# A gated mix of linear attention and a squared-ReLU block: another way to sum the keys over the partitions

## The chip, the cores and the metric

One core of one Trainium2 chip. The metric is the device time of one execution in microseconds (us). The kernel before takes 435.01 us, the median of three runs (434.67, 435.01 and 435.04).

## The reference, cut to what is computed

Everything is float32. `x` is 2048 tokens by 448 features, there are 16 heads of 28 features, and the hidden layer has 1792 units.

```python
g = sigmoid((x * gate_w).sum(-1, keepdims=True))
q, k, v = split(x @ wqkv)                        # 16 heads of 28
phi = lambda t: where(t > 0, t + 1, exp(t)) + 1e-6
pq, pk = phi(q), phi(k)
kv = einsum("bhsd,bhse->bhde", pk, v)
z  = einsum("bhsd->bhd", pk)                     # the sum of the keys over all tokens
num = einsum("bhqd,bhde->bhqe", pq, kv)
den = einsum("bhqd,bhd->bhq", pq, z)[..., None] + 1e-6
a = (num / den) @ wo
h = relu(x @ w1 + b1) ** 2
b = h @ w2 + b2
return g * a + (1 - g) * b
```

The change is about `z`: 448 numbers, each a sum over 2048 tokens.

## The kernel before

Tokens are handled in four blocks of 512 (`b` from 0 to 3), hidden units in 14 tiles of 128 (`f` from 0 to 13). The kernel makes two passes over the blocks. The first pass (`for b in range(1, NB)`, with block 0 written out ahead of it) does hidden tiles 0 to 6. For each tile, `up` multiplies `x` by `w1` into the PSUM tile `h_ps`, `hidden` applies ReLU and the square (ACT, into `hr`) and splits the result into a high and a low half (DVE, into `hh` and `hl`), and `down` multiplies these by `w2` into `o_ps`, one tile later. Every float32 product is made from such halves: high by high, high by low, low by high.

In the same pass `keys` makes the keys of 128 tokens at a time, and POOL adds them up in `ksum`, 128 partitions by 448. So `ksum` holds, on each partition, the sum over those tokens that fell on this partition; what is left is a sum over the 128 partitions. `gram` makes products of `x` with the keys; DVE adds them up in the four tiles `gsum`. `z` itself is needed in the second pass as `zc`, 128 partitions by 4: a column of feature sums for each of the four groups `c` into which the query features are ordered.

`key_sums` is called in block 3 at `f == 5`. POOL lays `ksum` out anew in `zk` (L375 to L377), and the same function then computes the gates (`gate`, L379 to L382). `kv_product` is called when block 3 has done tile 7, the first of the second pass. Its first lines sum over the partitions on TensorE (PE): each of the four 128 by 128 pieces of `zk` is loaded as the weights (L398) and multiplied by a tile of ones two columns wide, `ones`. These are plain float32 products, which the profile shows as two weight loads and two matmuls each. L400 copies the result from PSUM into `zc`. Then come the sixteen products of `gsum` with the value weights `wv` (L404), their masked copy `kv_raw` (L407) and the second pass, where `queries` uses `zc` (L466, L468) for the denominators.

Order. PE, ACT and DVE run their instructions in the order of the program text (`manual_schedule`). The order on POOL's queue and on SP's, which issues nearly all loads (L58), is fixed when the kernel is built, by a planner with a cost model; each queue then runs in that order, and an instruction that waits holds up those behind it. Work tiles come from one pool of 15 slots of 2 KB a partition (`slot`), handed out anew as they come free, so an added tile moves later tiles to other slots and with it what they wait for. The PSUM tiles of tag "mm" take turns in two banks; `z_ps` is one of them.

The part of the loop where the call stands:

```python
            if b == 3:
                ...
                if f >= 3:
                    split_w2(NH + f - 3)
                if f == 5:
                    key_sums()
                if f >= 5:
                    load_kv(2 * f - 10)
                    load_kv(2 * f - 9)
```

Of the kernel before, what the change touches and what calls it, by code (L numbers as in the profile page):

```python
# [7 lines left out]
F = mybir.dt.float32  # L8
R = mybir.dt.float32r
AF = mybir.ActivationFunctionType  # L10
ALU = mybir.AluOpType
# [4 lines left out]
P = 128  # L16
# [6 lines left out]
NJ = D // JE  # L23
# [7 lines left out]
def gated_mix_kernel(ctx: ExitStack, tc: tile.TileContext, xw, xt, xn, wk, wq, wv, wo, w1a, w1b, w2, b1, b2, gw,  # L31
                     hmask, kvmask, halves, out):
    nc = tc.nc
    act, dve, pool, pe, sp = nc.scalar, nc.vector, nc.gpsimd, nc.tensor, nc.sync

    keep = ctx.enter_context(tc.tile_pool(name="keep", bufs=1))
# [7 lines left out]
    mm_p = ctx.enter_context(tc.tile_pool(name="mm_p", bufs=2, space=PSUM))  # L44
# [3 lines left out]
    def bank(name):  # L48
        turn[0] ^= 1
        return ms_p.tile([P, 512], F, name=name, tag=f"ms{turn[0]}")  # L50
# [3 lines left out]
    def slot(shape, dt, name):  # L54
        return work.tile(shape, dt, name=name, tag="s", bufs=NSLOT)

    def load(dst, src):
        sp.dma_start(out=dst, in_=src)  # L58
# [45 lines left out]
    def load_x(b, c):  # L104
        x_raw[b, c] = slot([P, TB], F, f"xr{b}_{c}")
        load(x_raw[b, c], xt[b, c])
# [4 lines left out]
    def split_x(b, c):  # L111
        if c == 0:
            xs[b] = new_x(b)
        (xh, xl), r = xs[b], x_raw[b, c]
        if c < 3:
            split_hi(act, xh[:, c], r)
            split_lo(dve, xl[:, c], r, xh[:, c])
        else:
            split_last(xh[:, 3], xl[:, 3], r, side)
# [28 lines left out]
    def load_w2(f):  # L148
        w2_raw[f] = slot([P, D], F, f"w2r{f}")
        load(w2_raw[f], w2[f])  # L150
# [8 lines left out]
    def load_xn(t):  # L159
        xn_raw[t] = slot([P, D], F, f"xnr{t}")  # L160
        load(xn_raw[t], xn[t])
# [28 lines left out]
        load_w1(0, 0, c)  # L190
    b1_s = keep.tile([P, NF], F, name="b1_s")
    half = keep.tile([P, 2], F, name="half")
    ones = keep.tile([P, 2], F, name="ones")
    logit = keep.tile([P, NT], F, name="logit")
    gate = keep.tile([P, 2, NT], F, name="gate")
    zc = keep.tile([P, 4], F, name="zc")
    load(b1_s, b1)
    load_w2(0)
    load_w2(1)
# [5 lines left out]
    b2_s = keep.tile([P, D], F, name="b2_s")  # L205
    gw_s = keep.tile([P, D], F, name="gw_s")
    hm = keep.tile([P, 8 + P], R, name="hm")[:, 8:]
    dve.memset(ones, 1.0)
    ksum = keep.tile([P, D], F, name="ksum")

    phase1 = ExitStack()
# [29 lines left out]
    def up(b, f):  # L241
        ps = mm_p.tile([P, 512], F, name=f"h_ps{b}_{f}", tag="mm")
        for c in range(4):
            up_chunk(ps, b, f, c)
        hidden(ps, b, f)
# [14 lines left out]
    def down(b, f, tiles=range(4), leave=0, end=NH - 1):  # L260
        h, lo = hs[f]
        w = w2_s[f]
        for i in tiles:
            if f % NH == 0:
                o_ps[i] = acc_p.tile([P, 512], F, name=f"o_ps{b}_{f}_{i}", tag="acc")
            cols = slice(i * P, (i + 1) * P)
            for n, (a, m) in enumerate([(h, w[:, 0]), (h, w[:, 1]), (lo, w[:, 0])]):
                owed.append((o_ps[i][:, :D], a[:, cols], m, f % NH == 0 and n == 0, f % NH == end and n == 2))
        pay(leave)

    def half_done(b):
        for i in range(4):
            dve.tensor_tensor(part[4 * b + i], o_ps[i][:, :D], b2_s, op=ALU.add)
# [56 lines left out]
    def gram(b, c):  # L330
        ps = bank(f"g_ps{b}_{c}")
        cs = slice(c * P, (c + 1) * P)
        terms = []
        for t in range(4 * b, 4 * b + 4):
            ph, pl, nh, nl = pend[t]
            terms += [(nh[:, cs], ph), (nh[:, cs], pl)] + ([(nl[:, cs], ph)] if c < 3 else [])
        products(ps[:, :D], terms)

        def after():
            if b == 0:  # L340
                gsum.append(tmp.tile([P, D], F, name=f"gsum{c}"))
                act.copy(gsum[c], ps[:, :D])
            else:
                dve.tensor_tensor(gsum[c], ps[:, :D], gsum[c], op=ALU.add)
        return [after]
# [5 lines left out]
    def load_wq(c):  # L351
        wq_raw[c] = slot([P, TB], F, f"wqr{c}")
        load(wq_raw[c], wq[c])
# [3 lines left out]
    def split_wq(c):  # L357
        raw = wq_raw.pop(c)
        split_hi(act, wq_s[:, c], raw)
        if c < 3:  # L360
            split_lo(dve, wq_s[:, 4 + c, :384], raw[:, :384], wq_s[:, c, :384])
        else:
            split_lo(dve, wq_s[64:, 3, :384], raw[64:, :384], wq_s[64:, 3, :384])
        second = [t[:, 384:].rearrange("p (j r) -> p j r", j=NJ)[:, :, 16:] for t in (wq_s[:, c], raw)]
        split_lo(dve, second[0], second[1], second[0])
# [1 line left out]

    zks = []  # L370

    def key_sums():
        zk = slot([P, 4, NJ, 32], F, "zk")
        ks = ksum.rearrange("p (j k) -> p j k", j=NJ)
        pool.memset(zk[:, 3], 0.0)  # L375
        pool.tensor_copy(zk[:, :3], ks[:, :, :96].rearrange("p j (c r) -> p c j r", c=3))
        pool.tensor_copy(zk[:, 3, :, :16], ks[:, :, 96:])  # L377
        zks.append(zk)
        act.activation(gate[:, 0], logit, AF.Exp, scale=-1.0)  # L379
        dve.tensor_scalar_add(gate[:, 0], gate[:, 0], 1.0)  # L380
        dve.reciprocal(gate[:, 0], gate[:, 0])
        dve.tensor_scalar(gate[:, 1], gate[:, 0], -1.0, 1.0, op0=ALU.mult, op1=ALU.add)  # L382
# [10 lines left out]

    def kv_product():
        kv_ps = bank("kv_ps")
        z_ps = mm_p.tile([P, 512], F, name="z_ps", tag="mm")
        for c in range(4):
            pe.matmul(z_ps[:, 2 * c:2 * c + 2], zks[0][:, c].rearrange("p j r -> p (j r)"), ones, start=True,  # L398
                      stop=True)
        dve.tensor_copy(zc, z_ps[:, 0:8:2])  # L400
        for j in range(NJ):
            js = slice(j * JE, (j + 1) * JE)
            for c in range(4):
                pe.matmul(kv_ps[:JE, js], wv_s[c][:, js], gsum[c][:, js], start=(c == 0), stop=(c == 3))  # L404
        raw = slot([P, D], F, "kv_raw")
        dve.memset(raw[96:], 0.0)
        dve.tensor_tensor(raw[:JE], kv_ps[:JE, :D], kvm[0], op=ALU.mult)  # L407
        return raw.rearrange("p (j k) -> p j k", j=NJ)
# [121 lines left out]
    def run_todo():  # L530
        now, todo[:] = sorted(todo, key=lambda step: step.__name__ == "join"), []
        for step in now:
            todo.extend(step() or ())
# [85 lines left out]
    for b in range(1, NB):  # L619
        for f in range(NH):  # L620
            leave = leaves[b][f]
            run_todo()
            up(b, f)
            if f == 0:
                down(b - 1, NH - 1)
                half_done(b - 1)
                if b == 1:
                    for c in range(1, 4):
                        todo += gram(0, c)
                        run_todo()  # L630
            else:
                down(b, f - 1, leave=leave)
            if f == 1:
                todo += late_keys
                run_todo()
            if f == 0:
                load_xn(4 * b)
            if f < 4:
                if f < 3:
                    load_xn(4 * b + f + 1)  # L640
                if f == 0 and leave:
                    late_keys = keys(4 * b, leave)
                else:
                    late_keys = []
                    todo += keys(4 * b + f)
            elif f < 6:
                todo += gram(b, f - 4)
            else:
                todo += gram(b, 2)
                run_todo()  # L650
                todo += gram(b, 3)
            if b + 1 < NB:
                if 1 <= f < 5:
                    load_x(b + 1, f - 1)
                if 3 <= f:
                    split_x(b + 1, f - 3)
            if b == 2:
                if f < 4:
                    load_wq(f)
                if 1 <= f < 5:  # L660
                    split_wq(f - 1)
                if f == 5:
                    raw = slot([P, P], F, "hmr")
                    pool.dma_start(out=raw, in_=hmask)
                    split_hi(act, hm, raw)
                    load(half, halves)
            if b == 3:
                if f < 4:
                    load_w1(1, 0, f)
                if f == 4:  # L670
                    for c in range(4):
                        split_w1(1, 0, c)
                if f >= 2:
                    load_w2(NH + f - 2)
                if f >= 3:
                    split_w2(NH + f - 3)
                if f == 5:
                    key_sums()
                if f >= 5:
                    load_kv(2 * f - 10)  # L680
                    load_kv(2 * f - 9)
# [160 lines left out]
```

## Time and profile before

| what | value |
| --- | --- |
| median of three runs | 435.01 us |
| profiled execution, first to last instruction (its span) | 432.7 us |
| what the median has beyond that span | 2.3 us |
| PE busy | 428.9 us, 99% of the span |
| DVE busy | 284.7 us, 66% |
| ACT busy | 174.8 us, 40% |
| POOL busy | 72.0 us, 17% |
| mean DMA rate | 67 GB/s |

The profile is of one further execution of the same program. PEld is the loading of weights into TensorE, which overlaps its matmuls. A row of the timeline gives the start in us, the busy time in us (of all instructions merged into the row), the engine, the line, the operation, output and input tiles, and shapes; in brackets the time that the engine stood idle before it and what ended that. A row of a window gives the stretch, its length, and the engine's busy time in it with the number of instructions. A row of the transfers gives the number of transfers, the size of one, and the median us from its issue to its landing. Line numbers are those of the kernel before.

### The profile page before, as it was taken

To read this page: it belongs to the slowest core of one execution; us is meant where nothing else is said; L and a number is where in the kernel's file an instruction comes from. 1 tells how busy PE (TensorE), PEld (TensorE's weight loads), DVE (VectorE), ACT (ScalarE), POOL (GpSimd) and SP (SyncE) were. 2 spreads that over 40 slices of the span, in tenths; PEclk is the share of its full clock that TensorE was granted. 3 is DMA by queue.
4 is the path that set the end of the run, shared out by engine and by line. 5 is a ranking of instruction groups with operands and counts; after the bars stand their busy time and mean duration, and the time that the engine had idled before them with its cause. 6 is when DMAs were issued, how large, how long until landed. Compare 5 with 4: busy or idle time off the path is not lost.

```text
span 432.7 us, 5576 instructions
## 1 busy us (share of the span) xinstructions
PE 428.9 (99%) x2058; PEld 380.6 (88%) x2058; DVE 284.7 (66%) x464; ACT 174.8 (40%) x304; POOL 72.0 (17%) x93
## 2 busy tenths in 40 slices
PE   9999999999999999999999999999999999999997
PEld 6889999898989899898898888988888888888986
DVE  5999518843499337884459777887653966457624
ACT  6855324521346133453145543444433534233421
POOL 0055006500065002540010441000100001000000
PEclk9999999999999999999999999999999999999999
DMA  8842302120232211223245321130101401002002
GB/s 284 240 134 63 96 0 71 24 68 5 65 89 63 68 45 48 66 59 110 65 117 144 72 63 38 63 120 0 26 0 46 139 0 27 0 0 86 0 2 85
DMA packets 18411, 29.11 MB, mean 67 GB/s; under 512 B 2896, under 2 KB 12736, under 8 KB 18384
## 3 DMA queue, kind: packets, MB, share of 16 engines
q1 hardware_dynamic: 16480, 26.46, 20.1%
q0 software_dynamic: 1760, 2.20, 2.3%
q8 instruction: 16, 0.26, 0.3%
q14 instruction: 11, 0.09, 0.1%
q10 hardware_dynamic: 144, 0.10, 0.1%
HBM read 22.43 MB, written 3.67 MB: 60 GB/s over the span
## 4 chain that ended last, share of the span: by engine, by line
PE 99%; DVE 0%; issue 0%
PE h_ps L229 32%; PE o_ps L254 31%; PE q_ps L84 8%; PE a_ps L84 8%; PE g_ps L84 8%; PE k_ps L254 8%; PE kv_ps L404 1%; PE warm_ps L177 1%; PE m_ps L84 1%; PE d_ps L84 0%; PE last L84 0%; PE h_ps L549 0%; PE z_ps L398 0%; DVE last L786 0%
## 5 line engine op out<-in xcount | busy, mean ns | idle before, releaser
L254 PE MATMUL o_ps<-w,hh 128*128 128x448 f32 x444 | 127.9, 362 | 0.0
L229 PE MATMUL h_ps<-xh,w 128*128 128x512 f32 x390 | 124.7, 390 | 0.0
L254 PEld LDWEIGHTS o_ps<-w,hh 128*128 128x128 f32 x444 | 83.2, 187 | 7.6
L229 PE MATMUL h_ps<-xl,w 128*128 128x512 f32 x224 | 86.7, 389 | 0.0
L229 PEld LDWEIGHTS h_ps<-xh,w 128*128 128x128 f32 x390 | 73.1, 188 | 14.7 <-DVE w L72 0.4
L254 PE MATMUL o_ps<-w,hl 128*128 128x448 f32 x222 | 80.4, 362 | 0.0
L233 ACT ACTIVATE hr<-h_ps,b_s 128x512 f32<-128x512 f32 x56 | 38.1, 680 | 85.8 <-PE h_ps L229 80.3
L69 DVE CAST hh<-hr 128x512 fp32r<-128x512 f32 x56 | 23.5, 420 | 61.3 <-ACT hr L234 61.1
L229 PEld LDWEIGHTS h_ps<-xl,w 128*128 128x128 f32 x224 | 42.0, 188 | 7.9
L254 PEld LDWEIGHTS o_ps<-w,hl 128*128 128x128 f32 x222 | 41.6, 188 | 3.7
L72 DVE TENSOR_TENSOR hl<-hr,hh 128x512 fp32r<-128x512 f32 x56 | 39.6, 707 | 3.4
L72 POOL TENSOR_TENSOR nl<-xnr,nh 128x384 fp32r<-128x384 f32 x16 | 17.2, 1075 | 119.0 <-ACT nh L65 118.9
L234 ACT ACTIVATE hr<-hr 128x512 f32<-128x512 f32 x56 | 35.4, 632 | 1.8
L84 PE MATMUL q_ps<-xh,wq_s 128*128 128x512 f32 x100 | 33.0, 389 | 0.0
L84 PE MATMUL a_ps<-m_s,qh 128*128 128x448 f32 x112 | 32.7, 362 | 0.0
L254 PE MATMUL k_ps<-wk_s,xh 128*128 128x448 f32 x112 | 32.7, 361 | 0.0
L475 POOL DMA_DIRECT2D qr<-qv x16 | 7.9, 503 | 124.3 <-ACT qv L472 94.5
L72 DVE TENSOR_TENSOR pl<-r,ph 128x448 fp32r<-128x448 f32 x16 | 23.7, 1479 | 0.0
L326 POOL TENSOR_TENSOR ksum<-ksum,r 128x448 f32<-128x448 f32 x15 | 23.3, 1554 | 1.1 <-DVE r L288 1.1
L84 PE MATMUL q_ps<-xl,wq_s 128*128 128x512 f32 x60 | 23.3, 389 | 0.0
L254 PE MATMUL k_ps<-wk_s,xl 128*128 128x448 f32 x64 | 23.2, 363 | 0.0
L84 PE MATMUL a_ps<-m_s,ql 128*128 128x448 f32 x64 | 23.2, 362 | 0.0
(118 smaller groups left out, 571.0 us busy)
## 6 DMA issues: line engine op xcount, KB each, us to landing
xr<-in_xt SPq DMA_DIRECT2D x27, 256.0 KB, 2.7
xnr<-in_xn SPq DMA_DIRECT2D x16, 224.0 KB, 2.6
out<-out SPq DMA_DIRECT2D x15, 224.0 KB, 2.0
w2r<-in_w SPq DMA_DIRECT2D x14, 224.0 KB, 2.7
w1r<-in_w1a SPq DMA_DIRECT2D x7, 256.0 KB, 2.8
w1r<-in_w1b SPq DMA_DIRECT2D x8, 192.0 KB, 3.3
m_s<-m POOLq DMA_DIRECT2D x12, 112.0 KB, 2.5
wqr<-in_wq SPq DMA_DIRECT2D x4, 256.0 KB, 2.7
```

Source lines behind the costliest of these rows:

```text
L69: eng.tensor_copy(hi, src)
L72: eng.tensor_tensor(lo, src, f32(hi), op=ALU.subtract)
L84: pe.matmul(out_ps, a, b, start=(i == 0), stop=(i == n - 1))
L177: pe.matmul(warm_ps[:, :256], warm[:, :P], warm, start=True, stop=True)
L229: pe.matmul(ps, a, m, start=(c == 0 and n == 0), stop=(c == 3 and n == 1))
L233: act.activation(r, ps, AF.Relu, bias=b1_s[:, f:f + 1])
L234: act.activation(r, r, AF.Square)
L254: pe.matmul(ps, a, m, start=start, stop=stop)
L326: pool.tensor_tensor(ksum, ksum, p, op=ALU.add)
L404: pe.matmul(kv_ps[:JE, js], wv_s[c][:, js], gsum[c][:, js], start=(c == 0), stop=(c == 3))
L475: pool.dma_start(out=r[p + 16:p + 32], in_=v[p:p + 16])
```

## The change

The four products with `ones`, the tile `z_ps` and the copy into `zc` go. In their place `key_sums` goes on, on DVE: it transposes each 32 by 32 block of `zk` into `zt` (128 by 512), and adds up the 32 values that now lie next to each other, so that each partition holds 16 sums over 32 partitions each. One transfer writes these to DRAM (`zd`, 512 pieces of 16 bytes), four transfers bring them back, one for each 32 partitions (`z4`, 128 pieces of 16 bytes each), so that the four partial sums of a feature lie on one partition. In the next tile, `add_z` adds them with two small DVE instructions. The layout of `zk` changes with it (POOL's three instructions stay), and the gates become a function of their own, called right behind.

In the built program, DVE's order is: the split of `w2` tile 9, transposition, addition, gates, `gsum[1]`, ..., `gsum[2]`, the split of `w2` tile 10, `add_z`, `gsum[3]`. SP's order is: the mask `kvm`, `wv[0]`, `wv[1]`, the store of `zd`, the four loads of `z4` (the first waits for the store to land), then `w2` tile 11, `wv[2]`, `wv[3]`. ACT's ReLU of tile 7 in block 3 writes a slot that `zk` held, and waits for the store of `zd`.

```diff
-    ones = keep.tile([P, 2], F, name="ones")
-    zc = keep.tile([P, 4], F, name="zc")
+    z4 = keep.tile([P, 4, 4], F, name="z4")
+    zc = z4[:, 0]
+    z_d = ctx.enter_context(tc.tile_pool(name="z_d", bufs=1, space=bass.MemoryType.DRAM))
-    dve.memset(ones, 1.0)
-    zks = []
     def key_sums():
-        zk = slot([P, 4, NJ, 32], F, "zk")
+        zk, zt = slot([P, NJ, 4, 32], F, "zk"), slot([P, 16, 32], F, "zt")
         ks = ksum.rearrange("p (j k) -> p j k", j=NJ)
-        pool.memset(zk[:, 3], 0.0)
-        pool.tensor_copy(zk[:, :3], ks[:, :, :96].rearrange("p j (c r) -> p c j r", c=3))
-        pool.tensor_copy(zk[:, 3, :, :16], ks[:, :, 96:])
-        zks.append(zk)
+        pool.memset(zk[:, :, 3], 0.0)
+        pool.tensor_copy(zk[:, :, :3], ks[:, :, :96].rearrange("p j (c r) -> p j c r", c=3))
+        pool.tensor_copy(zk[:, :, 3, :16], ks[:, :, 96:])
+        dve.transpose(zt.rearrange("p a s -> p (a s)"), zk.rearrange("p j c r -> p (j c r)"))
+        zr = zk.rearrange("p j c r -> p (j c r)")[:, :16]
+        dve.tensor_reduce(zr, zt, axis=mybir.AxisListType.X, op=ALU.add)
+        zd = z_d.tile([NJ, P, 4], F, name="zd")
+        load(zd.rearrange("j p c -> p j c"), zr.rearrange("p (j c) -> p j c", c=4))
+        for j in range(NJ):
+            load(z4[32 * j:32 * j + 32], zd[j].rearrange("(i r) c -> r i c", i=4))
+
+    def add_z():
+        dve.tensor_tensor(z4[:, :2], z4[:, :2], z4[:, 2:], op=ALU.add)
+        dve.tensor_tensor(zc, zc, z4[:, 1], op=ALU.add)
+
+    def gates():
         act.activation(gate[:, 0], logit, AF.Exp, scale=-1.0)
     def kv_product():
         kv_ps = bank("kv_ps")
-        z_ps = mm_p.tile([P, 512], F, name="z_ps", tag="mm")
-        for c in range(4):
-            pe.matmul(z_ps[:, 2 * c:2 * c + 2], zks[0][:, c].rearrange("p j r -> p (j r)"), ones, start=True,
-                      stop=True)
-        dve.tensor_copy(zc, z_ps[:, 0:8:2])
         for j in range(NJ):
 ...
                 if f == 5:
                     key_sums()
+                    gates()
+                if f == 6:
+                    add_z()
```

## The prediction

> **What bounds the kernel.** I read the page's busy times and its chain first, then the waits of PE, then the timeline of PE and its weight loads around the place of the change.
>
> ```profile
> span 432.7 us, 5576 instructions
> PE 428.9 (99%) x2058; PEld 380.6 (88%) x2058; DVE 284.7 (66%) x464; ACT 174.8 (40%) x304; POOL 72.0 (17%) x93
> PE 99%; DVE 0%; issue 0%
> PE warm_ps L177 <- PEq L834: 0.8, 1, 0.8
> ```
>
> PE is busy for 99% of the span, the chain that ended last runs through PE for 99%, and PE's waits hold one row only: 0.8 us at the very start. PE's stream has no hole that a better order elsewhere could close, so the time falls by what is taken out of the stream and rises by what makes PE wait. An edit on DVE, POOL or SP counts for nothing unless it makes PE wait.
>
> ```profile
> 216.29 0.39 PE L84 MATMUL q_ps<-xh,wq_s 128*128 128x512 f32 x1
> 216.51 0.95 PE L398 MATMUL z_ps<-ones,zk 128*128 128x2 f32 x8
> 217.32 3.38 PE L404 MATMUL kv_ps<-gsum,wv 128*112 128x112 f32 x32
> 220.47 0.48 PE L229 MATMUL h_ps<-xh,w 128*128 128x512 f32 x1
> 216.29 1.08 PEld L398 LDWEIGHTS z_ps<-ones,zk 128*128 128x128 f32 x8
> 216.52 0.19 PEld L398 LDWEIGHTS z_ps<-ones,zk 128*128 128x128 f32 x1
> 217.29 0.47 PEld L404 LDWEIGHTS kv_ps<-gsum,wv 128*112 128x112 f32 x4
> 217.32:220.47 3.15, 3.15 (x35) 1.00 0.47 145
> ```
>
> The eight matmuls of the key sums stand between the last query product and the `kv` products, from 216.51 to 217.32: 0.81 us. The `kv` products that follow take 3.15 us for 32, 0.098 each. The clock granted there is 1.00.
>
> **What goes.** A matmul two columns wide has almost nothing to stream; the weight loads set the pace. The first `z` load starts at 216.29, beneath the last query matmul, and costs nothing; the second starts only at 216.52; the first `kv` load starts at 217.29. Without `z`, the first `kv` load takes the free place at 216.29 and the second starts at 216.52. Before, the second `kv` load starts one step behind the first, at 217.29 + 0.098 = 217.39. So the `kv` loads, and all of PE behind them, come 217.39 - 216.52 = 0.87 us earlier. The plainer sum, first `kv` matmul from 217.32 to 216.51, gives 0.81. I take 0.87, since the loads set the pace, and keep 0.81 as the other end.
>
> The Trainium skill speaks against that saving in one place: "TensorE: Matmul & The Clock Gate", section "Back-to-back issue gap", lets matmuls of up to 64 columns follow each other after about 25 ns, which as an estimate makes the eight worth 0.2 us. The rows disagree with it: seven steps lead from the second `z` load at 216.52 to the first `kv` load at 217.29, 0.11 us each.
>
> DVE loses the `zc` copy and a memset at the start, neither on the chain. The bank of `z_ps` falls out of the turn of the "mm" banks; the next tile then waits for the one that was freed two tiles ago, as elsewhere.
>
> **What comes, on DVE.** Transposition, addition and `add_z` have no row before; these are the rows near them and the places that they land in.
>
> ```profile
> 199.38 0.17 DVE L380 TENSOR_SCALAR gate<-gate 128x16 f32<-128x16 f32 x1
> 200.93 0.62 DVE L344 TENSOR_TENSOR gsum<-g_ps,gsum 128x448 f32<-128x448 f32 x1 [0.89 <-PE g_ps L84]
> 204.80 0.43 DVE L69 CAST hh<-hr 128x512 fp32r<-128x512 f32 x1 [3.25 <-ACT hr L234]
> 205.26 0.69 DVE L72 TENSOR_TENSOR hl<-hr,hh 128x512 fp32r<-128x512 f32 x1
> 209.83 0.62 DVE L344 TENSOR_TENSOR gsum<-g_ps,gsum 128x448 f32<-128x448 f32 x1 [0.44 <-PE g_ps L84]
> 213.70 0.43 DVE L69 CAST hh<-hr 128x512 fp32r<-128x512 f32 x1 [3.25 <-ACT hr L234]
> 190.00 1.57 DVE L72 TENSOR_TENSOR pl<-r,ph 128x448 fp32r<-128x448 f32 x1
> 192.24 0.70 POOL L377 COPY zk<-ksum 128x64 f32<-128x64 f32 x1
> ```
>
> POOL has `zk` ready at 192.94, long before 199.38, where the transposition takes the place of the gates: it waits for nothing. On 128x512, DVE instructions take from 0.43 (the cast) to 0.69 (`hl`); the slowest large one here is 1.57 (while POOL is busy too). I take 0.69 each, as both new ones read all 512 values: 1.4 us, with ends 0.9 and 3.1. The sums are then ready at 200.8 (200.3 to 202.5). The gates and the second `gsum` addition move back by 1.4, less the 0.89 of idle ahead of that addition: about 0.5. The next work, `hh` at 204.80, comes after 3.25 us of idle, which swallows that, and the upper end too (199.38 + 3.1 + 0.7 for the gates + 0.62 = 203.8). Nothing on PE needs the late addition before the `kv` products. So: zero, by that idle time.
>
> `add_z` stands at 209.4, behind the split of a `w2` tile and ahead of the last `gsum` addition at 209.83. It is two instructions of the gates' size, 2 x 0.17 = 0.34 us. The added wait is here: behind it on DVE stand that addition, for which the `kv` products wait, and `hh` of tile 7, whose products PE reaches only after the next `up`, which begins at 220.47. PE wants the addition by 216.51, so the data may land until 216.51 - 0.62 - 0.34 = 215.5 without cost.
>
> **What comes, on SP and in the transfers.** The tiny transfers have no like before; the bounds come from the smallest ones there are and from a two-hop sum.
>
> ```profile
> half<-in_halves SPq DMA_DIRECT2D x1, 1.0 KB, 6.2
> qr<-qv SPq DMA_DIRECT2D x16, 32.0 KB, 2.2
> out<-last SPq DMA_DIRECT2D x1, 128.0 KB, 1.8
> wv<-in_wv SPq DMA_DIRECT2D x4, 224.0 KB, 2.5
> L58 SPq DMA_DIRECT2D qr<-qv x16: 512/587/2074, 222.5 to 359.5; - x16
> 196.52 0.33 SPq L58 DMA_DIRECT2D w2r<-in_w  x1
> 198.99 0.83 SPq L58 DMA_DIRECT2D wv<-in_wv  x2
> 212.32 0.69 ACT L233 ACTIVATE hr<-h_ps,b_s 128x512 f32<-128x512 f32 x1 [7.08 <-PE h_ps L229]
> ```
>
> Storing `zd`: 1.8 us by the output's last piece, 6.2 by `half`, 128 pieces of 8 bytes, which was issued at 12 us into a start full of loads. The queue is nearly empty at 201, so I take 2.2 (`qr`). The four loads back are issued 0.59 apart, and the last lands 2.2 after its issue (ends 1.8 and 6.2). Likely: 200.8 + 2.2 + 3 x 0.59 + 2.2 = 207.0. Lower end: 200.3 + 1.8 + 1.8 + 1.8 = 205.7. Upper end: 202.5 + 6.2 + 1.8 + 6.2 = 216.7. The likely value is 2.4 us ahead of `add_z` at 209.4 and 8.5 ahead of 215.5. Cost: zero.
>
> The loads behind them on SP, `w2` tile 11 (issued at 196.52 before) and the last two `wv` (198.99), now go out after the fourth load back, from about 205.4: the last at 206.6, landing 2.5 later at 209. The `kv` products want the last `wv` at about 216.8. At the upper ends, SP is free of the loads back at 202.5 + 6.2 + 4 x 0.59 = 211.1, and the last `wv` lands by 215: still in time. `w2` tile 11 is split on ACT behind the ReLU at 212.32. That ReLU also waits for the store, likely landed at 203.0, at the latest at 208.7: no wait.
>
> **The sum.** 0.87 out of PE's stream, nothing added: the span goes from 432.7 to 431.8, and with the 2.3 us by which the median of the runs (435.01) lies above this execution's span, 434.1 us.
>
> **The rivals.**
>
> *The sums come back late (slower).* DVE stands in `add_z`, the last `gsum` addition is late, and PE waits ahead of the `kv` products. It decides from a landing at 215.5; each us beyond costs one. For it speaks the size of the pieces: the store has 512 of 16 bytes, four times as many as `half`. If that made the store twice `half`'s 6.2 and the loads as slow as `half`, the data would land at 200.8 + 12.4 + 1.8 + 6.2 = 221.2, PE would start 221.2 + 0.96 - 216.51 = 5.65 late, and the net would be +4.8: 439.8. It is slower than before from a landing at 216.4. Against it: `half` was slow in a crowded queue. The Trainium skill's "DMA: Bandwidth & Descriptors", section "Rules for kernel authors", is on its side: many small transfers should be made one, since under 64 KB mostly overhead is paid; the 6.2 us for 1 KB agrees.
>
> *The pairs are cheap and the `kv` products keep the start-up cost.*
>
> ```profile
> 216.51 0.28 PE L398 MATMUL z_ps<-ones,zk 128*128 128x2 f32 x2
> 216.54 0.36 PE L398 MATMUL z_ps<-ones,zk 128*128 128x2 f32 x2
> ```
>
> The first two `z` matmuls start 0.03 apart (216.51, 216.54). Eight at that pace are 0.24 us: 434.8. Against it: the other six intervals fill 0.78 of the 0.81. This is about what the 25 ns of the Trainium skill's "TensorE: Matmul & The Clock Gate", section "Back-to-back issue gap", would give.
>
> *The saving is handed back later.*
>
> ```profile
> DVE  5999518843499337884459777887653966457624
> ```
>
> In the slice from 227 to 238 us DVE is busy for 90% or more. If DVE paced PE there, PE's earlier start would end in a wait, and the time would stay at 435.0. Against it: DVE's work there begins with products of PE, so it shifts along; and no wait of PE shows after the start.
>
> **How the numbers follow.** Forecast as worked out: 0.78, at 434.1. Late sums 0.10, cheap pairs 0.05, handed back 0.07. The range takes in 0.4 us on either side of the forecast, for the spread of the runs (434.67 to 435.04), and reaches up to the two cases without a gain: 433.7 to 435.1. The bound of 0.2% is 0.87 us, about what a measurement of this kernel can tell from no change, and the forecast lies right on it. The three runs' mean is 434.91, below the median, so a reading of the change tends to come out a little larger than 0.87: of the 0.78 I give 0.54 to faster and 0.24 to within the bound. With the two gainless cases, same is 0.36; slower is the late sums, 0.10.
>
> **What would show it.** Right: no L398 in PE, the first `kv` matmul right behind the last query matmul, 0.22 after its start, PE's waits still one row of 0.8, DVE's `add_z` without idle ahead of it that a transfer ended, and a span of about 431.8. The transposition and the addition between 0.4 and 0.8 us each, the `z4` loads landed by 207. Wrong: a row of PE waiting for `gsum` or `wv`, a DVE wait for `z4` past 215.5, or a first `kv` load that starts as late as before.

## The result, and the profile after

The changed kernel takes 434.38 us, the median of eleven runs (433.56 to 434.66). The kernel before, beside it, takes 435.04 us. The ratio is 0.9982, with a 95% interval of 0.9973 to 0.9990. So the change makes the kernel faster by 0.18%, clear of the scatter of the runs, but by less than the 0.2% from which the prediction speaks of faster. The forecast was 434.1, in a range of 433.7 to 435.1.

The page of the changed kernel, its busy times, the chain, and the waits of PE:

```profile
span 432.1 us, 5571 instructions
PE 428.1 (99%) x2050; PEld 380.2 (88%) x2050; DVE 286.3 (66%) x466; ACT 175.0 (40%) x304; POOL 72.0 (17%) x93
PE 99%; DVE 0%; issue 0%
PE warm_ps L177 <- PEq L843: 0.8, 1, 0.8
```

PE has eight matmuls and eight loads fewer, and still no wait but the one at the start. The timeline of PE and of its weight loads at the place of the change:

```profile
216.39 0.39 PE L84 MATMUL q_ps<-xh,wq_s 128*128 128x512 f32 x1
216.62 3.31 PE L410 MATMUL kv_ps<-gsum,wv 128*112 128x112 f32 x32
219.69 0.48 PE L229 MATMUL h_ps<-xh,w 128*128 128x512 f32 x1
216.39 3.35 PEld L410 LDWEIGHTS kv_ps<-gsum,wv 128*112 128x112 f32 x32
```

The first `kv` load lies beneath the last query matmul, where the first `z` load lay. From the start of the last query matmul to the next `up` it is 219.69 - 216.39 = 3.30 us; before it was 220.47 - 216.29 = 4.18. That is 0.88 us gone. The first `kv` matmul starts 0.23 us after the last query matmul (216.39 to 216.62); before, 1.03 us lay between them (216.29 to 217.32).

The timeline of DVE, with what was added:

```profile
199.48 0.70 DVE L377 STREAM_TRANSPOSE zt<-zk 128x512 f32<-128x512 f32 x1
200.22 0.69 DVE L379 TENSOR_REDUCE zk<-zt 128x16 f32<-128x512 f32 x1
201.39 0.62 DVE L344 TENSOR_TENSOR gsum<-g_ps,gsum 128x448 f32<-128x448 f32 x1
204.91 0.43 DVE L69 CAST hh<-hr 128x512 fp32r<-128x512 f32 x1 [2.90 <-ACT hr L234]
209.41 0.16 DVE L386 TENSOR_TENSOR z<-z 128x8 f32<-128x8 f32 x1
209.60 0.16 DVE L387 TENSOR_TENSOR z<-z 128x4 f32<-128x4 f32 x1
209.93 0.62 DVE L344 TENSOR_TENSOR gsum<-g_ps,gsum 128x448 f32<-128x448 f32 x1 [0.17 <-PE g_ps L84]
```

The transposition and the addition take 0.70 and 0.69 us, the idle time ahead of `hh` shrinks from 3.25 to 2.90, and `add_z` (L386, L387) follows the work ahead of it without a wait: no bracket stands behind it. The last `gsum` addition waits for its product, not for `add_z`, and starts at 209.93 as against 209.83. The issues on SP's queue, and the transfers with their median us to landing:

```profile
200.97 0.39 SPq L58 DMA_DIRECT2D zd<-zk  x1
203.73 2.77 SPq L58 DMA_DIRECT2D z<-zd  x4
206.59 0.38 SPq L58 DMA_DIRECT2D w2r<-in_w  x1
207.07 0.85 SPq L58 DMA_DIRECT2D wv<-in_wv  x2
z<-zd SPq DMA_DIRECT2D x4, 2.0 KB, 2.2
zd<-zk SPq DMA_DIRECT2D x1, 8.0 KB, 2.7
```

The store is issued at 200.97, the loads back from 203.73 on, and the loads that stand behind them go out at 206.6 and later, ten and eight us later than before. No wait of PE comes of it.

### The profile page after: what moved, and what is told of

It reads as the page before. It is cut to its first block, busy times and chain, and to the rows that moved or that the text cites. A ratio compares the mean times of both kernels' runs of the same rounds, so it can differ in the third digit from the quotient of the medians.

```text
span 432.1 us, 5571 instructions
## 1 busy us (share of the span) xinstructions
PE 428.1 (99%) x2050; PEld 380.2 (88%) x2050; DVE 286.3 (66%) x466; ACT 175.0 (40%) x304; POOL 72.0 (17%) x93
## 4 chain that ended last, share of the span: by engine, by line
PE 99%; DVE 0%; issue 0%
PE h_ps L229 32%; PE o_ps L254 31%; PE q_ps L84 8%; PE k_ps L254 8%; PE a_ps L84 8%; PE g_ps L84 8%; PE warm_ps L177 1%; PE kv_ps L410 1%; PE m_ps L84 1%; PE d_ps L84 0%; PE last L84 0%; PE h_ps L555 0%; DVE last L795 0%
```

## The experiments

Theory A: the time falls by what the matmuls of the key sums took from PE's stream, all else is hidden. Rivals: the added work has a cost of its own, the pairs are cheap, the sums come late, the saving is handed back later. (A pair is one weight load and one matmul; each product of the key sums is two pairs.) The runs scatter by about 1 us, so beside the medians two rows of each timeline are compared: the first `k_ps` matmul, some 15 us after the start, and the last matmul of all. What lies between them, from start to start, is called the stream here: what PE does once it has started.

**The change again, and the removal alone.**

```diff
 # e1_no_z, against before
-        z_ps = mm_p.tile([P, 512], F, name="z_ps", tag="mm")
-        for c in range(4):
-            pe.matmul(z_ps[:, 2 * c:2 * c + 2], zks[0][:, c]..., ones, start=True, stop=True)
-        dve.tensor_copy(zc, z_ps[:, 0:8:2])
+        dve.memset(zc, 1.0)
```

> The changed kernel itself, beside the three below on one chip. If PE's stream alone decides: 0.88 us under the kernel before (the profile of the change had the query product to the next up at 3.30 us instead of 4.18), so 434.1 to 434.2 against 435.0, ratio 0.9980. If the 0.12 us that its profile lost in the first 10 us belongs to the change: about 0.75 under, ratio 0.9983.

> The kernel before without the eight matmuls of the key sums and the copy; the sum over the partitions is left out, a constant stands for it. If what is added on DVE, SP and in the transfers is fully hidden: the same time as the changed kernel, 0.88 us under before. If the added work costs something: faster than the changed kernel by that much. If the pairs are cheap and the kv products carry a start-up cost: only 0.2 us under before.

Measured: the changed kernel again 434.09 us, ratio 0.9983 (0.9974 to 0.9991); the removal alone 433.86, ratio 0.9978 (0.9969 to 0.9987); the intervals overlap. The span and the two rows, first of the kernel before, then of the changed kernel, of its repetition, and of the removal alone:

```profile
span 432.7 us, 5576 instructions
14.82 0.57 PE L254 MATMUL k_ps<-wk_s,xh 128*128 128x448 f32 x2
429.40 0.27 PE L84 MATMUL last<-w,hh 128*128 128x192 f32 x1
```

```profile
span 432.1 us, 5571 instructions
14.92 0.57 PE L254 MATMUL k_ps<-wk_s,xh 128*128 128x448 f32 x2
428.64 0.27 PE L84 MATMUL last<-w,hh 128*128 128x192 f32 x1
```

```profile
span 432.8 us, 5571 instructions
15.61 0.57 PE L254 MATMUL k_ps<-wk_s,xh 128*128 128x448 f32 x2
429.33 0.27 PE L84 MATMUL last<-w,hh 128*128 128x192 f32 x1
```

```profile
span 432.0 us, 5561 instructions
14.97 0.57 PE L254 MATMUL k_ps<-wk_s,xh 128*128 128x448 f32 x2
428.69 0.27 PE L84 MATMUL last<-w,hh 128*128 128x192 f32 x1
```

Between the rows: 414.58 us before, and 413.72, 413.72 and 413.72 in the other three. So the change takes 0.86 us out of the stream, and inside the stream its new way of making the sums costs nothing.

Ahead of the stream, runs of one program differ: it starts at 14.92 and at 15.61 for the same kernel. In the repetition ACT's first split of `x` began at 6.59 and waited for a load; in the first profile it began at 5.53. The 0.10 us by which the first profile started later than the kernel before (14.92 against 14.82) is no part of the change that these runs can show.

Behind the stream the change does cost something. From the start of the last matmul to the end of the span it is 432.7 - 429.40 = 3.3 us before and 3.3 in the removal alone (432.0 - 428.69), but 3.5 in the changed kernel and its repetition (432.1 - 428.64, 432.8 - 429.33). To three digits the traces have 3.31 to 3.32 in the four kernels without the five added transfers (before, and the runs e1, e3 and e9), and 3.48 to 3.50 in the changed kernel, its repetition, and the five runs built on it with the same transfers (e2, e4, e5, e10 and e11).

The records of SP's semaphore instructions, which the views leave out, show why. Each transfer counts its landing on one of a row of semaphores, and at its end the program waits on SP for these, one after the other in a fixed order, some 0.06 us each where nothing is awaited. The last transfer of all, a piece of the output, lands 2.4 us after the last matmul started, in every one of the fourteen traces. Before, its semaphore is the last to be waited for. In the changed kernel it is one that is waited for earlier, and three more waits follow: 3 x 0.06 = 0.18 us. The added transfers moved it. So this is a cost of the new way, though an accidental one: two more copies (e6 below) leave one wait behind it and 3.37 us in all, four (e7, e8) leave seven and 3.74.

By the traces the change is thus worth 0.86 - 0.18 = 0.68 us, a ratio of 0.9984, and the removal alone 0.86, a ratio of 0.9980. The medians are in line with that (0.9982 and 0.9983, and 0.9978), but their intervals are too wide to tell the two apart.

**Both ways at once.** The old matmuls put back into the changed kernel, their result unread:

```diff
 # e2_both, against the changed kernel
+    ones = keep.tile([P, 2], F, name="ones")
+    zo = keep.tile([P, 4], F, name="zo")
...
+        for c in range(4):
+            pe.matmul(z_ps[:, 2 * c:2 * c + 2], zks[0][:, c]..., ones, start=True, stop=True)
+        dve.tensor_copy(zo, z_ps[:, 0:8:2])
```

> The changed kernel with the old matmuls put back beside the new way (their result goes to a tile that nothing reads). If only PE's stream counts: the time of before, ratio 1.000. If the added DVE work and transfers cost something of their own: above before by that.

Measured: 439.48 us, ratio 1.0108 (1.0092 to 1.0123). Neither theory said this. PE has no wait here but the one at the start, and the eight matmuls take their 0.81 us; but most of the large products are slower, from the first pass on, and the stream is 418.94 us long. A group of the page, in the changed kernel and in this one:

```profile
L254 PE MATMUL o_ps<-w,hh 128*128 128x448 f32 x444 | 127.8, 362 | 0.0
```

```profile
L257 PE MATMUL o_ps<-w,hh 128*128 128x448 f32 x444 | 129.3, 366 | 0.0
```

A new theory: the two added tiles take 64 bytes a partition, and move the tiles of the same pool behind them (`x`, `w1`, `w2`, the key weights) by 64 bytes against the work slots of the other pool, which stay. Two kernels tell it apart: both ways without moving anything, and the move without both ways.

```diff
 # e4_both_in_place, against e2_both
-    half = keep.tile([P, 2], F, name="half")
+    half8 = keep.tile([P, 8], F, name="half")
+    half, ones, zo = half8[:, :2], half8[:, 2:4], half8[:, 4:]
...
-    ones = keep.tile([P, 2], F, name="ones")
-    zo = keep.tile([P, 4], F, name="zo")
 # e5_pad64, against the changed kernel
+    pad = keep.tile([P, 16], F, name="pad")
...
+    dve.memset(pad[:, :2], 1.0)
```

> The double kernel of e2_both once more (old matmuls and new way, the old result unread), but with its tile of ones and its result tile put into the unused rest of the tile half, so that no tile in SBUF lies elsewhere than in the changed kernel. If e2_both's 4.5 us come from the 64 bytes by which its two added tiles moved the tiles behind them: the time of before, ratio 1.000 (the matmuls give back the 0.88). If they come from doing both: 439.5 again.

> The changed kernel with one more, nearly unused tile of 64 bytes a partition behind z4, which moves the tiles behind it as in e2_both; nothing else. If the place of the tiles is the cause: e2_both less 0.88, 438.6, with a mean step of the o_ps matmuls near 203 ns instead of 200.5 from the first pass on. If not: 434.1, the time of the changed kernel.

Measured: 434.86 us, ratio 0.9998 (0.9989 to 1.0007), for both ways in place; 438.65 us, ratio 1.0087 (1.0073 to 1.0101), for the move alone. The group in the first and in the second:

```profile
L256 PE MATMUL o_ps<-w,hh 128*128 128x448 f32 x444 | 127.8, 362 | 0.0
```

```profile
L256 PE MATMUL o_ps<-w,hh 128*128 128x448 f32 x444 | 129.3, 366 | 0.0
```

Worked out from all starts of these matmuls and their `hl` partners, the mean step from one to the next is 203.9 ns with the move, 200.5 without (not the 203.1 that an expectation below has). Not every product slows alike: with 64 bytes the steps of `a_ps` go from 199.9 to 204.1 ns, of `q_ps` from 226.6 to 229.4, of `h_ps` from 226.9 to 228.4, of `k_ps` only from 199.8 to 200.1. Both points of the new theory hold. The eight matmuls alone bring the stream back to that of before (414.59 us against 414.58), so the gain is additive, and 64 bytes of layout cost five times what the change gains. How far it depends on the size of the move, two more pads show.

> The changed kernel with the added tile 32 bytes a partition in size in place of e5_pad64's 64. If any move of these tiles against those of the other pools costs what 64 bytes cost: 438.6. If the place of the changed kernel is only one of several and not the best: under 434.1. No theory says which; the mean step of the o_ps matmuls (200.5 ns, and 203.1 with 64 bytes) tells it.

> The same with 128 bytes. If the cost of a move repeats with a period of 128 bytes or a part of it: 434.1, the time of the changed kernel. If it does not: 436 to 440, as with 64.

Measured: 441.17 us, ratio 1.0148 (1.0131 to 1.0165), for 32 bytes; 438.15 us, ratio 1.0077 (1.0062 to 1.0092), for 128. Each of the three moves costs: between the two rows 4.33 us for 64 bytes, 6.63 for 32, 3.84 for 128. So there is no period of 128 bytes, and none of the three is better than the place that the changed kernel has. Why the place matters stays open, and so does whether it is the place of these tiles as such or their distance from those of the other pools. The two tiles that the change removes and enlarges happen to leave it as it was: 32 bytes for `ones` and 32 for `zc` before, 64 for `z4` after. The removal alone, which keeps the old tiles, and the changed kernel have the same stream of 413.72 us.

**The price of a pair.** The eight matmuls four times over, with 2 columns and with 48 (`wide`, 48 columns of ones in the tile `side`, whose size stays):

```diff
 # e3_z_x4, against before
-        for c in range(4):
+        for c in [0, 1, 2, 3] * 4:
 # e9_z_x4_wide, against e3_z_x4
-    dve.memset(ones, 1.0)
+    wide = side56[:, 8:56]
+    dve.memset(wide, 1.0)
...
-            pe.matmul(z_ps[:, 2 * c:2 * c + 2], zks[0][:, c]..., ones, ...)
+            pe.matmul(z_ps[:, 48 * c:48 * c + 48], zks[0][:, c]..., wide, ...)
-        dve.tensor_copy(zc, z_ps[:, 0:8:2])
+        dve.tensor_copy(zc, z_ps[:, 0:192:48])
```

> The kernel before with the eight matmuls done four times over (32 in place of 8). If each costs the pace of its weight load, 0.112 us: 24 x 0.112 = 2.7 us more, 437.7, ratio 1.0062. If narrow matmuls are paced at the 0.03 us of the first interval: 0.7 us more, ratio 1.0017.

> e3_z_x4 with 48 columns of ones in place of 2 (written into an unused part of another tile, so nothing moves). If the weight loads set the pace: the same 0.109 us a pair, 3.5 us for the 32. If the width counts: up to 24 times more streaming shows, over 4 us. And if the clock that fell to 0.62 behind the 32 narrow matmuls fell because the array had too little to do: with 48 columns it stays nearer to 1 and the time is below e3_z_x4's 439.3, down to 437.7; if it falls for another reason, 439.3 again.

Measured: 439.29 us, ratio 1.0106 (1.0089 to 1.0124), with 2 columns; 437.68, ratio 1.0064 (1.0048 to 1.0081), with 48. The timeline of PE and windows with the granted clock (the column behind the count), for 2 columns:

```profile
216.84 3.63 PE L398 MATMUL z_ps<-ones,zk 128*128 128x2 f32 x32
220.33 5.00 PE L404 MATMUL kv_ps<-gsum,wv 128*112 128x112 f32 x32
225.09 0.48 PE L229 MATMUL h_ps<-xh,w 128*128 128x512 f32 x1
220.50:221.00 0.50, 0.50 (x7) 1.00 0.00 0
221.50:222.00 0.50, 0.50 (x4) 0.50 0.81 133
224.00:224.50 0.50, 0.50 (x5) 0.50 0.00 0
224.50:225.00 0.50, 0.50 (x7) 0.99 0.00 0
```

and for 48:

```profile
217.00 3.67 PE L400 MATMUL z_ps<-side,zk 128*128 128x48 f32 x32
220.51 3.36 PE L406 MATMUL kv_ps<-gsum,wv 128*112 128x112 f32 x32
223.64 0.48 PE L231 MATMUL h_ps<-xh,w 128*128 128x512 f32 x1
220.33:222.70 2.37, 2.37 (x26) 1.00 0.35 91
```

The 32 pairs take 220.33 - 216.84 = 3.49 us with 2 columns and 220.51 - 217.00 = 3.51 with 48: 0.11 us each. The width costs nothing, the weight load sets the pace, and the cheap pairs are ruled out. The Trainium skill's "TensorE: Matmul & The Clock Gate", section "LDWEIGHTS (loading the stationary operand)", has columns divided by 1.2 in ns, 107 for 128, and the 109 and 110 ns measured here agree.

The other 1.6 us of the first kernel is the clock. It has 3.5 us of matmuls two columns wide, and some 0.7 us after their end, at about 221.0, the granted clock falls to 0.50 and stays there until 224.5, so that the `kv` products take 225.09 - 220.33 = 4.76 us in place of 3.15. With 48 columns it stays at 1.00. The fall does not come in every execution: of the five of this kernel, one had a mean clock of 1.000 and took 438.14 us, three had 0.995 or 0.996 and took 439.14 to 439.35, and one had 0.991 and took 440.82; the four with 48 columns all had 1.000 and took 437.56 to 437.71. So PE's busy share, which is full in both, does not decide. That the work in the array does is the reading that fits, from two widths. Part 1 of the same page of the Trainium skill, "The HAM clock gate", has a half-rate state and an activity window of 3413 ns; the stretch here, from about 221.0 to 224.5, agrees.

**How late the sums may come.** More copies from DRAM to DRAM between the store and the loads back:

```diff
 # e6_hops2, against the changed kernel; e7_hops4 has range(4)
+        for hop in range(2):
+            last = zd
+            zd = z_d.tile([NJ, P, 4], F, name=f"zd{hop}")
+            load(zd, last)
 # e8_hops4_late, against e7_hops4
-                if f == 6:
-                    add_z()
...
                     split_kv(raw)
+                    add_z()
```

> The changed kernel with two more copies from DRAM to DRAM between the store of the sums and their loads; each should take about 2.8 us from issue to the next issue, as the store did, so the sums land near 214 and add_z stands idle for some 4 us. If the limit is where the prediction put it (a landing by 215.5 costs nothing): 434.1, the time of the changed kernel. If the wait in add_z already costs something: up to 4 us more.

> The same with four more copies: the sums land near 219.5. If add_z holds up the last gsum addition and with it the kv products: PE waits from 216.6 to about 219.5 + 0.96, 3.8 us, and the time is 438, with a row of PE waiting for gsum. If z is not missed before the first use of zc near 230: 434.1.

> The kernel with four more copies, but with add_z moved behind the split of the kv product on DVE, just ahead of its first use. If the cost of four copies comes from DVE's order alone: back to 434.1, the time of the changed kernel. If it comes from SP, whose later loads stand behind the copies: as slow as with add_z in its old place, about 438.

Measured: two copies 434.37 us, ratio 0.9985 (0.9976 to 0.9994); four copies 435.16, ratio 1.0008 (0.9999 to 1.0017); four copies and a late `add_z` 434.60, ratio 0.9994 (0.9985 to 1.0003). DVE with two copies:

```profile
212.58 0.17 DVE L390 TENSOR_TENSOR z<-z 128x8 f32<-128x8 f32 x1 [2.62 <-DMA z<-zd]
```

DVE and PE with four, and PE's row of waits:

```profile
216.71 0.17 DVE L390 TENSOR_TENSOR z<-z 128x8 f32<-128x8 f32 x1 [7.15 <-DMA z<-zd]
217.00 0.62 DVE L344 TENSOR_TENSOR gsum<-g_ps,gsum 128x448 f32<-128x448 f32 x1
217.67 3.40 PE L414 MATMUL kv_ps<-gsum,wv 128*112 128x112 f32 x32 [0.82 <-DVE gsum L344]
PE kv_ps L414 <- DVE gsum L344: 0.8, 1, 0.8
```

With four and the late `add_z`, DVE and the two rows of PE:

```profile
222.26 0.17 DVE L390 TENSOR_TENSOR z<-z 128x8 f32<-128x8 f32 x1
15.12 0.57 PE L254 MATMUL k_ps<-wk_s,xh 128*128 128x448 f32 x2
428.84 0.27 PE L84 MATMUL last<-w,hh 128*128 128x192 f32 x1
```

With two copies DVE stands in `add_z` for 2.62 us, and PE's stream is 413.72 us long, as without. With four it stands for 7.15, the `kv` products start 0.96 us after the data (216.71 to 217.67), and the stream is 1.08 longer. The four copies were expected to cost more: they were issued 2.4 us apart on average, not 2.8, and the loads back had landed 3.3 us after the first of them was issued (213.37 to 216.71), not some 4.6 as in the changed kernel, so the data came at 216.7 and not at 219.5, and 3.8 us of waiting became 1.

With `add_z` moved, the stream is 413.72 again with the same four copies: DVE's order made the wait. What a late load on SP would cost is not tested by this, for in all three kernels with copies SP's order came out anew too. The last two loads of `wv`, which in the changed kernel stand behind all that was added, go out ahead of the loads back, here ahead of the last two copies as well:

```profile
206.01 0.38 SPq L58 DMA_DIRECT2D wv<-in_wv  x1
209.64 2.32 SPq L58 DMA_DIRECT2D zd<-zd  x2
213.31 1.86 SPq L58 DMA_DIRECT2D z<-zd  x4
```

The second of the two goes out at 207.18. By its runs alone this kernel could not be told from before. Its shorter stream and its longer end, 3.74 us against 3.31, leave 0.86 - 0.43 = 0.43 us, a ratio of 0.9990, which lies within the interval measured.

## Why the prediction was right

- **The sum.** The saving in PE's stream was put at 0.87 us with 0.81 as the other end; it is 0.88 at its place and 0.86 over the stream. The step that gave 0.87, a weight load that hides beneath a wide matmul and one that does not, holds: the first `kv` load took over the free place. The 25 ns for narrow matmuls would have left most of the saving out.
- **Nothing added.** This holds for PE's waits, but not for the whole program. The prediction looked at what makes PE wait and not at the end of the program, where the added transfers cost 0.18 us. The span came out at 432.1 and not at 431.8 for that and for a start 0.10 us later. The time stayed in the range because the term that was left out is small.
- **DVE.** The two instructions were taken at 0.69 us each from other 128x512 rows, and are 0.70 and 0.69; `add_z` at 0.34, and is 0.32. The idle time named as cover was the cover.
- **The transfers.** The store was put at 2.2 us and took 2.7; the loads back were put 0.59 apart and were issued over 2.77 us, as one issue alone took up to 1.4. The last lands at about 208.3 by the median, not at 207.0, 1.1 us ahead of `add_z` instead of 2.4. The terms were too small, and the `z4` loads had not landed by 207 as the list of signs says; the cover was large enough.
- **The limit.** A landing up to 215.5 was said to be free, and each us beyond to cost one, through 0.96 us of DVE work. The two and the four copies lie on either side, and the 0.96 was measured. The rival of late sums is a real mechanism that this change does not reach.
- **The rivals of cheap pairs and of a saving handed back** are out: by the repeated matmuls, and by the stream, which is shorter by the whole saving up to the last matmul. A fifth of it is lost behind that, by another way than the rival's, which had PE wait for DVE.
- **The chances.** More was given to faster than to within the bound, and the first comparison fell at 0.18%, just within it. The forecast did lie on the bound; that the reading would tend to come out larger than 0.87, argued from the mean of three runs, did not hold. With the cost at the end the traces give 0.16%, so within the bound was the likelier side. The repetition, at 0.17%, agrees; the removal alone, which has no such cost, is at 0.22%. That the repetition's median, 434.09, meets the forecast almost to the digit is luck: single profiles of one kernel start up to 0.7 us apart (14.92 and 15.61).

## What to carry to other kernels

Where PE is busy without a gap, a narrow product costs its weight load, 0.11 us for 128 columns (the same here for 2 and for 48 streamed columns), and a plain float32 product pays it twice; work moved from there into another engine's idle time takes exactly that out of PE's stream, if the wait it brings stands where the queue behind it has slack. Before an edit is blamed or praised for a per cent, compare the tiles' places in memory with those before: a tile of 32 bytes more cost 1.5% here. Where runs scatter by more than the effect, compare two marks inside the trace beside the whole time, and then look at what lies outside the marks: here a fifth of the gain was lost behind the last one.

## What the runs showed of the hardware that was not expected

- Moving one pool of tiles by 32, 64 or 128 bytes against the others slowed most of the large matmuls throughout: between the first `k_ps` matmul and the last matmul of all, 413.72 us became 420.35, 418.05 and 417.56, at a granted clock of 1.00 and with no wait of PE between the two.
- After 3.5 us of matmuls two columns wide the granted clock was halved for some 3.4 us in the profiled execution, though PE shows as fully busy; one of the five executions kept it. 48 columns at the same pace did not halve it in any of four.
- At its end the program waits for the semaphores of its transfers one after the other, 0.06 us each. Which of them the last output transfer has changed with the transfers added (none, five, seven, nine) and was the same in all kernels with the same number; the span ends 3.31 us after the last matmul's start where it is waited for last, and 3.37, 3.49 or 3.74 where one, three or seven waits follow.
- A store of 512 pieces of 16 bytes lands after 2.7 to 2.9 us, a copy of 8 KB within DRAM after 2.2 to 2.5, loads of 128 such pieces after 1.7 to 2.2 (medians of a run): near the 1.8 to 2.2 us of `out` and `qr` before, and far from the 6.2 us that one of 1 KB took in the crowded first microseconds.
